# Gate products with 32 weight columns held still, conversion work behind attention on VectorE, and a longer hold for urgent work

## The chip, the cores and the metric

The kernel runs on one NeuronCore of one Trainium2 chip. Times are device microseconds (us) of that core. Engines are TensorE (PE, with its weight loads PEld), VectorE (DVE), ScalarE (ACT), GpSimd (POOL) and SyncE (SP), which issues most DMAs; POOL issues the indirect ones.

## The reference

Three layers follow one another on 3072 tokens of width 512.

```python
# 1. attention, 4 x 8 heads x 768 x 64: a local window of |i-j| < 16 and 24 block keys (max of k, mean of v over 32)
a = softmax(concat([masked scale*q@k.T, scale*q@k_sum.T + log(32)]))
x = (a @ concat([v, v_sum])).reshape to (3072, 512)
# 2. experts: 8 of them, each takes exactly 384 tokens
logits = x @ w_gate                       # 3072 x 8
# all (token, expert) pairs in falling order of logit; a token goes to the first expert that still has room
out[mask_e] = relu(x[mask_e] @ w1[e]) @ w2[e]
# 3. a dense block
h = ((out @ W1) * (out @ W2)) @ w3 @ w_out
```

## The kernel before

The program is one long stream of operations that a planner in the kernel (class `Plan`) puts in order before anything is emitted. Each operation has a due time (`with at(t)`), a duration from `cost()`, and dependencies. `run()` walks a clock: an engine that is free takes the ready operation with the earliest due time, provided that its buffers are free. Operations recorded under `urgent()` are in `hots`; an engine doesn't start other work that would still run when an urgent operation, known to become ready within `HOLD`, wants it. Buffers are given back some time after their last use: `REL` (100 ns) in general, but longer for VectorE operations that are not urgent and touch a tile named `rt` (factor on `SAFE`, 600 ns). On TensorE a change of the array's mode (full, or narrow column tiles) costs `PEN` in due time. What comes out is a fixed order for each engine; on the chip each engine runs its own list in order.

Stages. **Attention**: 16 units `u` of one batch and two heads, each with three groups `group(G)`; on TensorE every group has scores, transposes of the exponentials, products with v, and transposes `xo` into `xt`. In each third group the gate logits are accumulated: `rt` collects `xt` times `wg`, 128 tokens by 8 experts in each of six tiles, over four units; then `LG` takes them. Beside this, `conv()` turns pieces of 64-bit float weights into float32 (two 512-column halves for each 128 rows): an absolute value and a rescaling on ScalarE, a clamp on GpSimd, a shift and a merge on VectorE, an integer addition on GpSimd. `split_sb` splits a float32 tile into a rounded part (ScalarE) and the rest (GpSimd by default); `split_ps` does the same out of PSUM with VectorE.

**Transition**: when the last logits are in `LG`, `routing(0)` finds the threshold of the first expert in six rounds (VectorE compares: `gq`; TensorE counts: `rt`; VectorE: `need`, `sat`, `ni`, `base`, `thr`, `pre`), then the list of its tokens (`idx`). `fold(i)` multiplies a transposed block of w3 (`mm<-ident,w`) by w_out (`ac<-wh,xh` and so on) and keeps the product; one fold may run before the last logits and seven run behind them, as TensorE's filler. In the same stretch the dense block's first two weight matrices are made ready: tiles `ab`, half of them reloaded from `abd` (`load_ab`), half converted there (`conv_ab`).

**Experts**: 8 times. Gather the tokens (`xg`, transposed and split into `xh`, `xl`), gather w1 (`ra`) and w2 (`st`, two buffers shared with the staging of `conv`), two layers (`mm<-xh,wh`, `ac<-hh,wh`), the dense block (`mm<-xh,ab`, `ac<-w,hh`) and a scatter, while `routing(e+1)` runs among the products.

`nc.bar` is the operation that closes attention's pool; code recorded after it sees `nc.bar` set, code before it sees `None`.

Of the kernel before, what the change touches and what calls it, by code (L numbers as in the profile page):

```python
# [8 lines left out]
F32 = mybir.dt.float32  # L9
F32R = mybir.dt.float32r  # L10
BF = mybir.dt.bfloat16
I32 = mybir.dt.int32
U32 = mybir.dt.uint32
AF = mybir.ActivationFunctionType
OP = mybir.AluOpType
# [84 lines left out]
class Plan:  # L100
# [130 lines left out]
    def run(self):  # L231
# [20 lines left out]
        t, order, ends, todo = self.clock, [], [], n - base  # L252
        busy = {e: 0.0 for e in ready}
        while todo:
            moved = False
            for e, (wait, q) in ready.items():
                while wait and wait[0][0] <= t:
                    i = heapq.heappop(wait)[1]
                    heapq.heappush(q, (ops[i][5], i))
                if self.free.get(e, 0.0) > t:  # L260
                    continue
                soon = min((w[0] for w in wait if w[1] in self.hots and w[0] < t + HOLD), default=None)
                skip, got = [], None
                if e == "tensor" and q:

                    q[:] = [(ops[i][5] + PEN * (i < self.bar and self.modes.get(i) != self.mode), i) for _, i in q]
                    heapq.heapify(q)
                while q:
                    x = heapq.heappop(q)
                    late = soon is not None and x[1] not in self.hots and t + ops[x[1]][6] > soon  # L270
                    if not late and all(self.room(b) for b in ops[x[1]][4]):
                        got = x[1]
                        break
                    skip.append(x)
                for x in skip:
                    heapq.heappush(q, x)
                if got is None:
                    continue
                i = got
                dur, post = ops[i][6], ops[i][7]  # L280
                for b in ops[i][4]:
                    self.take(b)
                if e == "tensor" and i < self.bar and self.modes.get(i) != self.mode:
                    self.mode = self.modes.get(i)
                    dur += SWITCH
                self.free[e], done = t + dur, t + dur
                busy[e] += dur
                if post:

                    self.dma = max(self.dma, done + DMA_LEAD) + post  # L290
                    done = self.dma + DMA_END
                    if e == "sync":
                        self.free[e] = max(t + dur, self.dma - DMA_AHEAD)
                slow = e == "vector" and i not in self.hots and any(b.name == "rt" for b in ops[i][3])
                heapq.heappush(ends, (done + (SAFE if slow else REL), i))
                order.append(i)
                self.done[i] = t
                todo -= 1
                moved = True
                for j in users.get(i, ()):  # L300
                    kind = ops[j][2][i]
                    if kind == 0:
                        settle(i, j, t)
                    else:
                        late = self.bar is not None and j > self.bar
                        safe = 0.0
                        if e != ops[j][0] and not late:
                            safe = SAFE_A.get(ops[j][0], SAFE_O) + (SAFE_D if post else 0.0)
                        elif e != "tensor" and ops[j][0] == "tensor":
                            safe = SAFE  # L310
                        if j in self.calms and e != ops[j][0]:
                            safe = max(safe, (CALM_D if post else CALM) * (0.3 if late else 1.0))
                        settle(i, j, done + safe + (0.0 if post else LAG[e].get(ops[j][0], 0.0)))
            if moved:
                continue
            nxt = [x for x in self.free.values() if x > t] + [w[0][0] for w, _ in ready.values() if w and w[0][0] > t]
            if ends:
                nxt.append(ends[0][0])
            assert nxt, "the plan is stuck"
            t = max(t, min(nxt))  # L320
            while ends and ends[0][0] <= t:
                i = heapq.heappop(ends)[1]
                for b in ops[i][3]:
                    b.uses -= 1
                    b.when = t
# [6 lines left out]
        for i in order:  # L332
            eng, fn, _, _, new, _, _, _ = ops[i]
# [8 lines left out]
       "vector": {"tensor": 150, "scalar": 128, "gpsimd": 156, "sync": 120, "vector": 127},  # L342
       "gpsimd": {"tensor": 143, "scalar": 76, "vector": 80, "sync": 240}}

HOLD = 150.0

CALM, CALM_D = 500.0, 2000.0

# [2 lines left out]
SAFE = 600.0  # L351

SAFE_A, SAFE_O, SAFE_D = {"tensor": 1200.0, "sync": 2000.0}, 200.0, 1500.0
REL = 100.0
# [92 lines left out]
def body(tc, q, k, v, w_gate, w1, w2, wa, wb, w3, wo, out):  # L447
# [5 lines left out]
    nc = Plan(tc.nc)  # L453
# [3 lines left out]
    E, _, F = w1.shape  # L457
    C = N // 128
    cap = N // E
    NT, FB, DB = cap // 128, F // 128, Dm // 128  # L460
    NB, NJ, HP = S // 32, S // 64, H // 2
# [8 lines left out]
    STEP, T0, TL, TE = 3.3, 243, 271, 87  # L470
    GATE, EARLY = 1, 0.0
    NF, TR, FT, FD = 1, 2, 245, 3
    NW, ND, AB0, ABD = 8, 2, 12, 3.9
    P_LD, P_MN, P_VL, P_PUT, P_VC, P_RL, P_TR, P_N = 24, 8, 14, 6, 11, 10, 10, 2
    P_ST, P_SC, P_C0, P_C1, P_CL, P_FO, P_FS = 8, 10, 10, 15, 6, 3, 5
    P_GA, P_SU, P_RW, P_W2, P_W20, P_RO, P_WC = 20, 16, 40, 16, 6, 15, 6
# [17 lines left out]
    ap_ = pool(att, "att")  # L494
    pp = pool(st, "ps", space=PSUM)
# [6 lines left out]
    with at(-8):  # L502
        jp = ap_.tile([128, 128], I32, name="jp")
        nc.gpsimd.iota(jp, pattern=[[1, 128]], base=0, channel_multiplier=-1)
        ident = cp.tile([128, 128], F32, name="ident")
# [63 lines left out]
    with at(10):  # L569
        triu = cp.tile([128, 128], BF, name="triu")  # L570
        nc.vector.tensor_scalar(triu, jp, 0.0, None, op0=OP.is_gt)
        LG = cp.tile([128, C, E], F32, name="LG")
        WG = ap_.tile([128, DB, E], F32, name="wg")
        nc.sync.dma_start(WG, w_gate.rearrange("(c p) e -> p c e", p=128))


    def split_sb(hi, lo, raw, eng=None):
        nc.scalar.activation(hi, raw, AF.Copy)
        (eng or nc.gpsimd).tensor_tensor(lo, raw, hi.bitcast(F32), op=OP.subtract)

    def split_ps(hi, lo, ps):
        nc.scalar.activation(hi, ps, AF.Copy)
# [11 lines left out]
    def stage():  # L594
        return ep.tile([128, 1024], F32, name="st", bufs=2, fifo=True)


    stages = []

    def conv(src, r, h, dst, t, raw=None):  # L600

        with at(t - P_CL):
            if raw is None:
                stages.append(ap_.tile([128, 1024], F32, name="sta", bufs=2, fifo=True) if len(stages) % 2 else stage())
                raw = stages[-1]
            nc.sync.dma_start(raw.bitcast(I32), src[r * 128:(r + 1) * 128, h * 512:(h + 1) * 512].bitcast(I32))
        with at(t), nc.patient():
            w = raw.bitcast(I32).rearrange("p (a b) -> p a b", b=2)
            lo, hi = w[:, :, 0], w[:, :, 1]
            c = ap_.tile([128, 512], F32, name="ca", bufs=1) if nc.bar is None and len(stages) % 4 == 0 else ep.tile([128, 512], F32, name="a", bufs=3)  # L610
            nc.scalar.activation(c, hi.bitcast(F32), AF.Abs)
            nc.scalar.activation(lo, lo.bitcast(U32), AF.Copy, scale=2.0 ** -29)
            nc.gpsimd.tensor_scalar(c, c, 122879.9921875, 2.0 ** -15, op0=OP.min, op1=OP.max)
            a = c.bitcast(I32)
            nc.vector.tensor_scalar(a, a, 5, 2, op0=OP.logical_shift_left, op1=OP.logical_shift_right)
            nc.vector.scalar_tensor_tensor(a, hi, -1073741824, a, op0=OP.bitwise_and, op1=OP.bitwise_or)
            f = dst if dst is not None else c
            nc.gpsimd.tensor_tensor(f.bitcast(I32), a, lo, op=OP.add)
        return f

    WO, W3, WF = {}, {}, {}
# [1 line left out]
    for j in range(FB):  # L623
        t = P_C0 + (215 - P_C1) * j / nconv
        f = conv(wo, j, 0, None, t)
# [11 lines left out]
    for n, (m, d, h) in enumerate((m, d, h) for m in range(2) for d in range(ND) for h in range(2)):  # L637
        t = P_C0 + (215 - P_C1) * (FB + 2 * NW + n) / nconv
        f = conv((wa, wb)[m], d, h, None, t)
# [24 lines left out]
    GT, XT, XO = {}, {}, {}  # L664
# [76 lines left out]
    def group(G):  # L741
        nonlocal gate

        u, g = divmod(G, 3)
        b, pr = divmod(u, HP)
        with at(STEP * G):
            ps = pp.tile([128, 4, WC], F32, name="ac", bufs=2)
# [12 lines left out]
        with at(STEP * G + Q_E):  # L760
            s = ap_.tile([128, 4, WC], F32, name="s", bufs=4)
            for i in range(4):
                nc.scalar.activation(s[:, i, :], ps[:, i, :], AF.Exp, bias=mx[:, i:i + 1])
        with at(STEP * G + Q_T):
# [4 lines left out]
            p = PT[G % 3]  # L769
            nc.scalar.activation(p[0:WC], pt, AF.Copy)  # L770
        with at(STEP * G + Q_V):
            po = pp.tile([128, 2, 2, 65], F32, name="ac", bufs=4, first=3)
            with nc.block():
                for a in range(2):
                    for h in range(2):
                        for b2 in range(2):
                            i = 2 * a + b2
# [23 lines left out]
        if g == 2:  # L801
            with at(STEP * G + P_SC):
                if pr == 0:
                    GT[b] = pp.tile([128, 6, E], F32, name="rt", fifo=True)
                with nc.block():
                    for i in range(3):
                        for t in range(2):
                            nc.tensor.matmul(GT[b][:, 2 * i + t], XT[u, i][:, t], WG[:, pr], start=(pr == 0 and i + t == 0),
                                             stop=(pr == HP - 1 and i + t == 3))
        if pr == HP - 1 and g == 2:  # L810
            with at(STEP * G + P_SC):
                nc.vector.tensor_copy(LG[:, 6 * b:6 * b + 6, :], GT[b])

    for u in range(NU):
        prep(u)
# [505 lines left out]
```

## Time and profile before

| | |
|---|---|
| median of 3 runs | 1032.13 us (1030.18 to 1032.99) |
| the profiled execution | 1025.71 us, span 1023.9 us, mean granted clock 0.982 |
| busy, share of the span | PE 94%, PEld 86%, DVE 59%, ACT 40%, POOL 31% |
| attention (to the last `LG` copy) | 0 to 229 us |
| transition (to the first product of expert 0) | 229 to 298 us |
| experts | 298 to 1024 us, a period of 90 us |

The profile gives the time, duration and name of each instruction, and for an engine's idle time what released it. The share of busy time is a mean over stages with different limits, so the stages are read one by one. [...]

### The profile page before, as it was taken

To read this page: it belongs to the slowest core of one execution; us is meant where nothing else is said; L and a number is where in the kernel's file an instruction comes from. 1 tells how busy PE (TensorE), PEld (TensorE's weight loads), DVE (VectorE), ACT (ScalarE), POOL (GpSimd) and SP (SyncE) were. 2 spreads that over 40 slices of the span, in tenths; PEclk is the share of its full clock that TensorE was granted. 3 is DMA by queue.
4 is the path that set the end of the run, shared out by engine and by line. 5 is a ranking of instruction groups with operands and counts; after the bars stand their busy time and mean duration, and the time that the engine had idled before them with its cause. 6 is when DMAs were issued, how large, how long until landed. Compare 5 with 4: busy or idle time off the path is not lost.

```text
span 1023.9 us, 17970 instructions
## 1 busy us (share of the span) xinstructions
PE 966.9 (94%) x6827; PEld 877.7 (86%) x6827; DVE 603.9 (59%) x1620; ACT 409.8 (40%) x961; POOL 321.5 (31%) x401
## 2 busy tenths in 40 slices
PE   6798989997989999999999999999999999999995
PEld 5688978775678899989989998998999899999994
DVE  5775576858877853882685388268538726323210
ACT  5786878864343233233223323222332323223211
POOL 9986466646623221041022104102210414001001
PEclk9998999998999999999999999999999999999998
DMA  8767778772141311040131105003110405101000
GB/s 235 193 181 204 207 210 257 208 232 112 32 164 42 125 52 52 1 165 31 33 121 54 52 2 165 32 32 111 65 52 1 165 21 165 42 11 52 1 1 31
DMA packets 81703, 100.06 MB, mean 98 GB/s; under 512 B 30416, under 2 KB 63696, under 8 KB 81616
## 3 DMA queue, kind: packets, MB, share of 16 engines
q1 hardware_dynamic: 68560, 52.76, 18.3%
q0 software_dynamic: 13056, 46.14, 13.6%
q8 instruction: 54, 0.88, 0.3%
q14 instruction: 33, 0.27, 0.1%
HBM read 81.81 MB, written 14.68 MB: 94 GB/s over the span
## 4 chain that ended last, share of the span: by engine, by line
PE 57%; issue 10%; DVE 7%; DMA 4%; ACT 2%; POOL 2%; POOLq 0%; ACTq 0%; SPq 0%; DVEq 0%
PE mm L395 32%; PE ac L395 23%; DMA ra<-in_moe_w_dram,iw 3%; PE rt L395 2%; POOL ra L1109 1%; DVE wl L395 1%; DVE gq L395 1%; DVE a L395 1%; DVE xl L395 1%; DMA abd<-ca 1%; ACT s L395 1%; DMA st<-in_moe_w_dram,iw 1%; DVE base L395 1%; ACT wh L395 1%; DVE pre L395 0%
## 5 line engine op out<-in xcount | busy, mean ns | idle before, releaser
L395 PE MATMUL mm<-xh,ab 128*128 128x384 f32 x1024 | 273.4, 338 | 0.0
L395 PEld LDWEIGHTS mm<-xh,ab 128*128 128x128 f32 x1024 | 185.5, 188 | 4.5 <-issue 3.3
L395 PE MATMUL mm<-xl,ab 128*128 128x384 f32 x512 | 174.4, 341 | 0.0
L395 PE MATMUL ac<-w,hh 128*128 128x512 f32 x384 | 123.6, 398 | 0.0
L395 DVE TENSOR_TENSOR a<-a,mm 128x384 f32<-128x384 f32 x64 | 35.2, 551 | 140.4 <-PE mm L395 117.9
L1109 POOL DMA_INDIRECT ra<-in_moe_w_dram,iw x32 | 31.4, 982 | 219.3 <-DVE go L395 190.9
L395 PEld LDWEIGHTS mm<-xl,ab 128*128 128x128 f32 x512 | 96.1, 188 | 3.0 <-DVE xl L395 1.1
L395 PE MATMUL mm<-xh,wh 128*128 128x384 f32 x256 | 88.1, 345 | 0.8 <-ACT xh L395 0.7
L395 PE MATMUL mm<-xl,wh 128*128 128x384 f32 x256 | 87.0, 340 | 0.0
L395 PE MATMUL ac<-hl,wh 128*128 128x384 f32 x256 | 87.0, 340 | 0.0
L395 PE MATMUL ac<-hh,wl 128*128 128x384 f32 x256 | 86.8, 339 | 0.0
L395 PE MATMUL mm<-xh,wl 128*128 128x384 f32 x256 | 86.6, 338 | 0.0
L395 ACT ACTIVATE a<-mm 128x384 f32<-128x384 f32 x64 | 31.3, 490 | 137.6 <-PE mm L395 137.6
L1109 POOL DMA_INDIRECT xg<-xd,idx x24 | 35.3, 1472 | 158.6 <-PE mm L395 119.4
L395 PE MATMUL ac<-hh,wh 128*128 128x384 f32 x256 | 84.5, 337 | 0.0
L1171 POOL DMA_INDIRECT out_dram<-a,idx x24 | 26.7, 1114 | 176.9 <-ACT a L395 173.7
L395 PEld LDWEIGHTS ac<-w,hh 128*128 128x128 f32 x384 | 70.9, 188 | 11.8
L395 ACT ACTIVATE hh<-a 128x384 fp32r<-128x384 f32 x64 | 33.5, 524 | 115.7 <-DVE a L395 115.7
L395 DVE TENSOR_TENSOR wl<-st,wh 128x512 fp32r<-128x512 f32 x64 | 44.0, 688 | 57.7 <-ACT wh L395 57.5
L395 PE MATMUL ac<-w,hl 128*128 128x512 f32 x192 | 76.4, 398 | 0.0
L395 DVE TENSOR_TENSOR wl<-ra,wh 128x512 fp32r<-128x512 f32 x64 | 43.9, 687 | 41.7 <-ACT wh L395 41.7
L395 ACT ACTIVATE wh<-ra 128x512 fp32r<-128x512 f32 x64 | 42.4, 664 | 62.2 <-PE mm L395 32.7
(271 smaller groups left out, 2078.8 us busy)
## 6 DMA issues: line engine op xcount, KB each, us to landing
st<-in_moe_w_dram SPq DMA_DIRECT2D x14, 512.0 KB
sta<-in_moe_w_dram SPq DMA_DIRECT2D x14, 512.0 KB
kn<-in_k_dram SPq DMA_DIRECT2D x32, 192.0 KB
qn<-in_q_dram SPq DMA_DIRECT2D x32, 192.0 KB
xd<-xo SPq DMA_DIRECT2D x16, 384.0 KB
vw<-in_v_dram SPq DMA_DIRECT2D x32, 176.0 KB
vw<-vs SPq DMA_DIRECT2D x64, 36.6 KB
st<-in_moe_w_out_dram SPq DMA_DIRECT2D x4, 512.0 KB
```

The lines of the kernel that those rows point to most:

```text
L395: return getattr(real_engine, method)(*map(real, a), **{k: real(x) for k, x in kw.items()})
L1109: nc.add("gpsimd", lambda: tc.nc.gpsimd.indirect_dma_start(out=real(dst), out_offset=None, in_=real(src), in_offset=bass.IndirectOffsetOnA ...
L1171: s = tc.nc.gpsimd.indirect_dma_start(out=out, out_offset=bass.IndirectOffsetOnAxis(ap=real(idx), axis=0), in_=real(o), in_offset=None)
```

## The change

1. The gate logits are computed with `wg` held still (each of the four 128-row pieces padded from 8 to 32 columns with zeros) and 256 tokens of `xt` streaming: three products for each unit, into three bands of 32 partitions. Before, six products held 128x128 of `xt` still and streamed 8 columns. After four units, ScalarE copies the 96 rows out (`lt`), TensorE transposes them in two pieces, and VectorE copies the first 8 columns of each band to `LG`.
2. Code recorded after `nc.bar` gives the rests of `split_sb` and the final addition of `conv` to VectorE. Its staging uses `st` alone, where `sta` (attention's pool) alternated with it.
3. `AB0`, the first due time of the `ab` work relative to `T0`, goes from 12 to 22. `HOLD` goes from 150 to 300 ns, and `rt` tiles of VectorE operations that are not urgent are given back after 1800 instead of 600 ns.

```diff
-                heapq.heappush(ends, (done + (SAFE if slow else REL), i))
+                heapq.heappush(ends, (done + (3 * SAFE if slow else REL), i))
...
-HOLD = 150.0
+HOLD = 300.0
...
-    NW, ND, AB0, ABD = 8, 2, 12, 3.9
+    NW, ND, AB0, ABD = 8, 2, 22, 3.9
...
-        WG = ap_.tile([128, DB, E], F32, name="wg")
-        nc.sync.dma_start(WG, w_gate.rearrange("(c p) e -> p c e", p=128))
+        WG = ap_.tile([128, DB, 32], F32, name="wg")
+        nc.gpsimd.memset(WG, 0.0)
+        nc.sync.dma_start(WG[:, :, 0:E], w_gate.rearrange("(c p) e -> p c e", p=128))
...
-        (eng or nc.gpsimd).tensor_tensor(lo, raw, hi.bitcast(F32), op=OP.subtract)
+        (eng or (nc.gpsimd if nc.bar is None else nc.vector)).tensor_tensor(lo, raw, hi.bitcast(F32), op=OP.subtract)
...
-                stages.append(ap_.tile([128, 1024], F32, name="sta", bufs=2, fifo=True) if len(stages) % 2 else stage())
+                stages.append(ap_.tile([128, 1024], F32, name="sta", bufs=2, fifo=True) if nc.bar is None and len(stages) % 2 else stage())
...
-            nc.gpsimd.tensor_tensor(f.bitcast(I32), a, lo, op=OP.add)
+            (nc.gpsimd if nc.bar is None else nc.vector).tensor_tensor(f.bitcast(I32), a, lo, op=OP.add)
...
-                    GT[b] = pp.tile([128, 6, E], F32, name="rt", fifo=True)
+                    GT[b] = pp.tile([128, 256], F32, name="rt", fifo=True)
                 with nc.block():
                     for i in range(3):
-                        for t in range(2):
-                            nc.tensor.matmul(GT[b][:, 2 * i + t], XT[u, i][:, t], WG[:, pr], start=(pr == 0 and i + t == 0),
-                                             stop=(pr == HP - 1 and i + t == 3))
+                        nc.tensor.matmul(GT[b][32 * i:32 * i + 32], WG[:, pr], XT[u, i].rearrange("p t s -> p (t s)"),
+                                         start=(pr == 0), stop=(pr == HP - 1))
         if pr == HP - 1 and g == 2:
             with at(STEP * G + P_SC):
-                nc.vector.tensor_copy(LG[:, 6 * b:6 * b + 6, :], GT[b])
+                lt = ap_.tile([96, 256], F32, name="lt", bufs=1)
+                nc.scalar.activation(lt, GT[b][0:96], AF.Copy)
+                ps = pp.tile([128, 2, 96], F32, name="mm", bufs=3)
+                for t in range(2):
+                    nc.tensor.transpose(ps[:, t, :], lt[:, t * 128:(t + 1) * 128], ident[0:96, 0:96])
+                nc.vector.tensor_copy(LG[:, 6 * b:6 * b + 6, :].rearrange("p (g t) e -> p g t e", t=2),
+                                      ps.rearrange("p t (g r) -> p g t r", r=32)[:, :, :, 0:E])
```

How the order of the engines moves is shown at three places. TensorE at the end of attention, before; `ac` with `xh`, `xl` is a fold, `rt<-wg,xt` a pair of gate products, `mm<-ident,w` a fold's transposes:

```order
L395 MATMUL ac_3477<-wl_1246,xh_3394 128x512
L395 MATMUL rt_3172<-wg_155,xt_3490 128x8 x2
L395 MATMUL rt_3172<-wg_155,xt_3508 128x8 x2
L395 MATMUL rt_3172<-wg_155,xt_3534 128x8 x2
L395 MATMUL ac_3477<-wh_1220,xl_3395 128x512
L395 MATMUL mm_3562<-ident_88,w_1_1496 128x128 x4
```

The same place with the change:

```order
L395 MATMUL ac_3382<-wh_1268,xl_3222 128x512
L395 MATMUL rt_3140<-xt_3437,wg_347 32x256
L395 MATMUL rt_3140<-xt_3465,wg_347 32x256
L395 MATMUL rt_3140<-xt_3483,wg_347 32x256
L395 MATMUL mm_3504<-ident_88,lt_3499 128x96 x2
L395 MATMUL mm_3526<-ident_88,w_1_1533 128x128 x4
```

Three products stand for six, and the two transposes of `lt` follow them at once, ahead of the next fold. The first fold's last product stands before the logits now.

VectorE in the second round of `routing(0)`, before (`a<-ab,a` is a conversion's merge, `w` a fold's result):

```order
L395 TENSOR_TENSOR gq_3697<-key_3574,thr_3692 128x768
L395 TENSOR_TENSOR gq_3705<-key_3574,thr_3692 128x768
L395 TENSOR_TENSOR w_1_3708<-ac_3598,w_1_3708 128x512
L395 TENSOR_TENSOR need_3738<-rem_1046,rt_3715 32x8 x2
L395 TENSOR_TENSOR sat_3743<-rt_3715,need_3738 63x8
L395 TENSOR_REDUCE ni_3754<-rt_3751 128x1
```

With the change (`ab` minus `ab` is the rest of a gate weight):

```order
L395 TENSOR_TENSOR gq_3621<-key_3509,thr_3616 128x768
L395 TENSOR_TENSOR gq_3631<-key_3509,thr_3616 128x768
L395 TENSOR_TENSOR ab_0_3537<-ab_0_3537,ab_0_3599 128x512
L395 TENSOR_SCALAR a_3628<-a_3628 128x512
L395 TENSOR_TENSOR need_3662<-rem_791,rt_3640 32x8 x2
L395 TENSOR_TENSOR sat_3669<-rt_3640,need_3662 63x8
L395 TENSOR_TENSOR w_1_3665<-ac_3564,w_1_3665 128x512
L395 TENSOR_REDUCE ni_3682<-rt_3679 128x1
```

A rest and a conversion's shift now stand between the comparison and `need`, and the fold's result after `sat`. From the `LG` copy to `idx` twelve such rests and additions are new in VectorE's list; a conversion and a half, and two folds' results, have left that stretch.

GpSimd as expert 0 begins, before (`xg` gathers tokens, `st` gathers w2, `a` is a conversion, `ab` a rest):

```order
L1109 DMA xg_4248<-xd,idx_4193 128x512
L1109 DMA st_4273<-in_moe_w_dram,iw_0_4049 128x1024
L395 TENSOR_SCALAR a_4378<-a_4378 128x512
L395 TENSOR_TENSOR a_4378<-a_4378,st_4336 128x512
L1109 DMA st_4428<-in_moe_w_dram,iw_0_4049 128x1024
L395 TENSOR_TENSOR ab_0_3730<-a_4378,ab_0_3713 128x512
```

With the change:

```order
L1115 DMA xg_4184<-xd,idx_4123 128x512
L1115 DMA st_4222<-in_moe_w_dram,iw_0_3974 128x1024
L1115 DMA st_4282<-in_moe_w_dram,iw_0_3974 128x1024
L395 TENSOR_SCALAR a_4417<-a_4417 128x512
L395 TENSOR_SCALAR a_4515<-a_4515 128x512
L395 TENSOR_SCALAR a_4552<-a_4552 128x512
L395 TENSOR_SCALAR a_4650<-a_4650 128x512
```

The fourth gather of w2 now goes ahead of all conversions, and four conversions stand here, where two stood: the other two were done in attention before, through `sta`. SP loads their four pieces last of all.

## Rows read from the trace of the kernel before

**Rows 1.** Busy time by stretch: us, PE, PEld, DVE, ACT, POOL, clock, DMA.
```profile
50.00:220.00 170.00, 156.85 (x1874) 138.76 (x1874) 116.05 (x235) 136.54 (x414) 110.09 (x151) 0.95 0.76 209
229.00:298.00 69.00, 57.56 (x321) 41.38 (x322) 61.85 (x143) 30.92 (x55) 38.62 (x32) 0.95 0.31 111
298.00:337.00 39.00, 36.62 (x228) 35.19 (x228) 26.83 (x86) 13.06 (x25) 7.73 (x7) 0.96 0.15 45
427.00:517.00 90.00, 89.49 (x548) 82.84 (x547) 55.80 (x176) 26.29 (x51) 16.18 (x17) 1.00 0.19 65
```
**Rows 2.** Timeline of PE in attention: start, us, instruction, count, idle before.
```profile
53.03 0.49 PE L395 MATMUL mm<-ident,qr 128*128 128x128 f32 x3
53.36 0.38 PE L395 MATMUL mm<-ident,xo 128*128 128x128 f32 x2
...
57.55 1.40 PE L395 MATMUL rt<-wg,xt 128*128 128x8 f32 x12
...
60.42 0.55 PE L395 MATMUL mm<-ident,kr 128*128 128x128 f32 x3
60.90 0.88 PE L395 MATMUL mm<-vw,ind 96*32 96x130 f32 x24
...
64.02 1.05 PE L395 MATMUL ac<-kw,qb 128*128 128x120 f32 x8
```
**Rows 3.** Timeline of DVE in `routing(0)`.
```profile
229.14 0.21 DVE L395 COPY LG<-rt 128x48 f32<-128x48 f32 x1 [3.95 <-PE rt L395]
...
236.47 1.18 DVE L395 TENSOR_SCALAR a<-a 128x512 int32<-128x512 int32 x1
...
239.84 0.91 DVE L395 SCALAR_TENSOR_TENSOR base<-tb,u 128x1 int32<-128x1 int32 x1
240.79 1.26 DVE L395 TENSOR_TENSOR thr<-js,base 128x64 int32<-128x64 int32 x1
241.97 1.26 DVE L395 TENSOR_TENSOR pre<-js,base 128x32 int32<-128x32 int32 x1
243.15 3.36 DVE L395 TENSOR_TENSOR gq<-key,thr 128x768 bf16<-128x768 f32 x2
...
250.81 0.16 DVE L395 SCALAR_TENSOR_TENSOR base<-ni,base 128x1 int32<-128x1 int32 x1
...
251.11 0.19 DVE L395 TENSOR_TENSOR pre<-js,base 128x32 int32<-128x32 int32 x1
251.22 0.95 DVE L395 TENSOR_TENSOR gq<-key,thr 128x768 bf16<-128x768 f32 x1
...
269.32 1.26 DVE L395 SCALAR_TENSOR_TENSOR base<-ni,base 128x1 int32<-128x1 int32 x1
...
287.58 0.15 DVE L395 SCALAR_TENSOR_TENSOR idx<-i 128x3 int32<-128x3 f32 x1
```
**Rows 4.** Timeline of POOL in the same stretch.
```profile
240.69 1.27 POOL L395 TENSOR_TENSOR ab<-ab,ab 128x512 fp32r<-128x512 f32 x1
241.92 1.26 POOL L395 TENSOR_TENSOR ab<-a,ab 128x512 fp32r<-128x512 f32 x1
```
**Rows 5.** Timeline of PE in the transition.
```profile
245.29 0.33 PE L395 MATMUL rt<-oh,gq 128*128 128x16 bf16 x6 [5.04 <-DVE gq L395]
...
297.77 1.41 PE L395 MATMUL mm<-xh,wh 128*128 128x384 f32 x3 [0.69 <-ACT xh L395]
```
**Rows 6.** Groups by line and shape: instruction, count, busy us, mean ns, idle before.
```profile
L395 DVE TENSOR_TENSOR wl<-st,wh 128x512 fp32r<-128x512 f32 x64 | 44.0, 688 | 57.7 <-ACT wh L395 57.5
L395 ACT ACTIVATE xt<-mm 128x256 f32<-128x256 f32 x48 | 19.3, 403 | 2.8 <-PE mm L395 2.7
L395 POOL TENSOR_TENSOR ab<-ab,ab 128x512 fp32r<-128x512 f32 x8 | 11.2, 1410 | 7.0 <-ACT ab L395 7.0
L395 POOL TENSOR_SCALAR a<-a 128x512 f32<-128x512 f32 x32 | 21.6, 679 | 28.0 <-ACT a L395 20.4 <-DVE thr L395 5.4 <-DVE rs L395 0.9
```
**Rows 7.** Timeline of ACT and of PE in expert 0.
```profile
318.56 1.15 ACT L395 ACTIVATE wh<-st 128x512 fp32r<-128x512 f32 x2 [4.67 <-DMA st<-in_moe_w_dram,iw]
322.22 0.31 PE L395 MATMUL rt<-oh,gq 128*128 128x16 bf16 x6 [1.36 <-DVE gq L395]
```

## The prediction

> **What bounds the kernel now.** I read the busy time by stretch first, then the engines' timelines in the stretches that are not full, then the groups of instructions for prices. The stretches [rows 1] show three regimes. In a steady expert TensorE is busy 89.49 of 90 us: nothing in the change alters its products, so 7 of the 8 periods are taken as they are. In attention (50 to 220 us) TensorE is busy 156.85 of 170 us, 92%, with ScalarE next at 136.54 us, 80%: here TensorE's own work sets the pace, not quite alone. In the transition (229 to 298 us) TensorE is busy 57.56 of 69 us and VectorE 61.85: the chain of `routing(0)` on VectorE is the longer one. It starts with the `LG` copy at 229.14 and gives `idx` at 287.58, 58.4 us later [rows 3]; the first product of expert 0 follows at 297.77, 10.2 us on [rows 5], behind the gather of tokens. The expert-0 stretch of 39 us has 2.4 us of idle TensorE (39.00 - 36.62) [rows 1].
>
> **The gate products.** A unit's batch takes 1.40 us on TensorE now [rows 2], in 12 records, which are six float32 products. It comes 16 times. What replaces it isn't in the trace, so I bound it by two rows. The block means use the same kind of narrow tile, 32 columns held still: 12 products of 130 columns, 1560 columns in all, take 0.88 us [rows 2]. Four bands work there, three will here; 3 x 256 = 768 columns cost 0.88 x 768/1560 x 4/3 = 0.58 us. If the bands do not overlap, the full-width float32 row decides: 4 products of 120 columns in 1.05 us [rows 2], so 768 columns cost 1.05 x 768/480 = 1.68 us.
>
> A switch between the full and the narrow form also shows: three transposes reach the next instruction after 0.33 us elsewhere (53.03 to 53.36), but after 0.48 us when the narrow means follow (60.42 to 60.90) [rows 2], 0.15 us. So a batch saves 1.40 - 0.58 - 0.15 = 0.67 us, 16 of them 10.7 us; at the other end it costs 1.68 + 0.15 - 1.40 = 0.43 us more, 6.9 us in all. I take the row of the means, because its instruction has the same narrow form. [...]
>
> What of 10.7 us reaches the end? TensorE was idle 8% of the stretch, and ScalarE at 80% goes to about 85% when the stretch shrinks. I pass on a good half: **-6 us**, with 0 and -10.7 as ends of this term if the tiles overlap. The clamp, addition and load of two conversions also leave attention for expert 0; they are off its critical engine there, so I give them nothing here.
>
> **The logits' way out.** Three of the four copies stand inside attention, with other work queued on TensorE between product and transpose. The last one is on the path: where `LG` followed the product at once, there are now a copy on ScalarE (0.40 us by the nearest row, `xt` with 256 columns [rows 6]), two transposes (0.33 us for three of 128 [rows 2], so about 0.25) and two more hand-overs. I put **+1 us** on it. TensorE stands still meanwhile, since the transposes are next in its list; ends +0.7 and +1.5.
>
> **The transition.** Between 236.47 and 269.32 eleven VectorE instructions of the chain and of the conversions (first and last shown, the worst four between) take 15.6 us [rows 3]. The same forms take 0.16 us (`base`), 0.19 (`pre`), 0.95 (`gq`) when nothing disturbs them [rows 3]; summed that way the eleven would take 4.4 us. Each long one ends with a two-input GpSimd instruction: `thr` at 240.79 and `pre` at 241.97 run beside `ab` at 240.69 and 241.92 [rows 3, 4]. So 11.2 us of the chain are waits for GpSimd. The costliest is the second round, where TensorE stands 5.04 us for `gq` [rows 5]. [...]
>
> The change takes those GpSimd instructions (1410 ns each [rows 6]) out of the stretch. In their place twelve of VectorE's own stand in the list from `LG` to `idx`, at 688 ns each (`wl`, same shape and operands [rows 6]): 12 x 0.69 = 8.3 us. One and a half conversions and two fold results leave it (some 2.9 us at 0.4 to 0.7 us each). One end: all that is added lies on the chain, -11.2 + 8.3 = -2.9 us. Other end: the added ones fill the places where VectorE waited for a count from TensorE, and the chain falls by 11.2 and nearly all the rest is free: -12 us. [...] I take **-9 us**: 69 becomes 60.
>
> Four clamps stay on GpSimd in this stretch (679 ns [rows 6]). [...]
>
> **Expert 0.** The wait of ScalarE for the fourth piece of w2, 4.67 us, and TensorE's 1.36 us behind it [rows 7] should go, since that gather is issued ahead of the conversions now. In its place VectorE gets two more whole conversions, and the additions and rests of four: 4 x 2 x 0.69 + 2 x 1.1 = 7.7 us in a stretch where it was busy 26.83 of 39 us [rows 1]. It becomes nearly full, in front of counts that TensorE waits for in order. I put **+1 us** (-2.4, all idle time gone, to +5). `HOLD` and the longer life of `rt` act only on the plan; with TensorE at 99% in the experts I give them zero, ends -1 and +2.
>
> **Sum.** -6 + 1 - 9 + 1 = -13 us. The profiled execution took 1025.71 us, its span and 1.8 us around it; it would become 1012.7. The median of the runs is 6.4 us longer (1032.13). I carry the difference over to the median: **1019 us**.
>
> **Rivals.**
> *Attention keeps its pace* (0.15). ScalarE, the loads and GpSimd set it, and TensorE only idles more. For it: ScalarE's 80%; against: TensorE's 92%. Then 1032.1 + 0 + 1 - 9 + 1 = 1025.
> *VectorE's newcomers take back the transition* (0.15). They stand in front of `need` and `ni` rather than beside a wait. For it: VectorE is busy 61.85 of 69 us; against: a good part of that was waiting. Term -2.9: 1025.
> *The bands do not overlap* (0.08), so the change does not do what it says: +6.9 in attention. For it: no row with 256 columns. Then 1032.1 + 6.9 + 1 - 9 + 1 = 1032, no change.
> *Slower: conversions block VectorE in expert 0* (0.10). Their four pieces go through the two `st` buffers behind w2, and VectorE's list has their shifts in front of `gq` and `hl`, for which TensorE waits. If each arrives as late as w2's fourth piece did, 4.67 us [rows 7], that is 18.7 us: 1032.1 - 6 + 1 - 9 + 18.7 = 1037. It decides for "slower" from 4.3 us a piece (to make up 14 us and 3 more). Against it: the loads are issued when w2's halves are split, several products ahead.
> *My forecast* has 0.52, with its own range 1012 to 1025.
>
> **How the numbers follow.** About 0.3%, 3 us, is what a measurement of this kernel can tell from no change. Forecast and the first two rivals lie below 1029: 0.82, of which I hold back 0.02 for their upper tails. The third gives 0.08, with a little from the others 0.09; slower 0.11. The range reaches down for the unknown costs (-10.7 and -12 together give 1011, with no loss in expert 0 1009) and up over the two rivals at 1025: 1009 to 1030.
>
> **What would show it.** The gate products in three records' worth of 256 columns at about 0.6 us a batch; the `LG` copy some 5 us earlier, near 224; in `routing(0)` `base`, `thr` and `pre` at 0.2 us each, no TensorE wait of 5 us, `idx` about 49 us behind `LG`; first product of expert 0 near 284; expert period 90.0 as before. The forecast is wrong if the batches still take 1.4 us, if VectorE waits in expert 0 for a conversion's shift, or if the stretch from `LG` to `idx` stays above 55 us.

## The result: 1002 us, and the profile after

The changed kernel takes 1002.35 us, the median of 4 runs (999.45 to 1003.75), beside 1031.16 (1028.75 to 1032.99) for 4 runs of the kernel before: ratio 0.9718, 95% interval 0.9687 to 0.9749. The forecast was 1019 us with a range of 1009 to 1030. The direction was right, and the time lies below the range: the gain is 29 us by the medians where I had 13.

The profiled execution took 999.45 us, with a span of 997.7, 26.2 us under the span before. (Both profiled executions are faster than their medians, that of the kernel before by 5.5 us and this one by 2.9, so the spans show a smaller gain.) The mean granted clock is 0.990 (before 0.982). TensorE is busy 95% of the span, VectorE 61%, ScalarE 41%, GpSimd 28%. Split at the same five points the 26.2 us are:

| stretch | before, us | after, us | difference | forecast |
|---|---|---|---|---|
| start to the last `LG` copy | 229.1 | 215.9 | -13.2 | -5 |
| `LG` copy to `idx` | 58.4 | 49.4 | -9.0 | -9 for both |
| `idx` to the first product of expert 0 | 10.2 | 11.3 | +1.1 | |
| from there to expert 0's first product with `ab` | 39.4 | 36.2 | -3.2 | +1 |
| from there to the end | 686.7 | 684.9 | -1.8 | 0 |

Busy time by stretch, after (us, then PE, PEld, DVE, ACT, POOL, and clock, DMA share, GB/s), against [rows 1]:

```profile
50.00:207.00 157.00, 141.97 (x1815) 117.93 (x1815) 111.71 (x223) 134.02 (x407) 103.31 (x135) 1.00 0.79 218
216.00:276.00 60.00, 54.31 (x310) 39.74 (x310) 55.76 (x150) 27.23 (x51) 15.22 (x15) 0.97 0.41 141
276.00:312.00 36.00, 34.51 (x218) 33.08 (x219) 30.83 (x83) 16.27 (x30) 3.45 (x5) 1.00 0.29 89
402.00:492.00 90.00, 89.99 (x550) 83.62 (x549) 56.37 (x179) 26.65 (x51) 14.75 (x17) 1.00 0.20 65
```

In attention the clock column reads 1.00 where it read 0.95. In a steady expert TensorE is busy 89.99 of 90 us where it was busy 89.49.

TensorE in attention, after (start, us, instruction, count), against the batch in [rows 2]:

```profile
55.63 0.88 PE L395 MATMUL mm<-vw,ind 96*32 96x130 f32 x24
56.32 0.61 PE L395 MATMUL rt<-xt,wg 128*32 128x256 f32 x6
56.86 0.98 PE L395 MATMUL mm<-ident,xo 128*128 128x128 f32 x4
...
213.06 0.63 PE L395 MATMUL rt<-xt,wg 128*32 128x256 f32 x6
214.56 0.39 PE L395 MATMUL mm<-ident,lt 96*128 96x96 f32 x2 [0.86 <-ACT lt L395]
214.78 1.04 PE L395 MATMUL mm<-ident,w 128*128 128x128 f32 x8
```

A batch is recorded with 0.61 us, and the next instruction starts 0.54 us behind its start. From 213.06 on stands the logits' way out: TensorE waits 0.86 us for ScalarE's copy `lt`, transposes it, and goes on with a fold.

VectorE from the last logits to the third round of `routing(0)`, after, against [rows 3]:

```profile
214.87 0.42 DVE L395 TENSOR_SCALAR ca<-ca 128x512 int32<-128x512 int32 x1
215.32 0.69 DVE L395 SCALAR_TENSOR_TENSOR ca<-sta,ca 128x512 int32<-128x512 int32 x1
215.93 0.20 DVE L395 COPY LG<-mm 128x48 f32<-128x48 f32 x1
...
225.47 0.16 DVE L395 SCALAR_TENSOR_TENSOR base<-tb,u 128x1 int32<-128x1 int32 x1
225.66 0.23 DVE L395 TENSOR_TENSOR thr<-js,base 128x64 int32<-128x64 int32 x1
225.81 0.19 DVE L395 TENSOR_TENSOR pre<-js,base 128x32 int32<-128x32 int32 x1
225.92 1.83 DVE L395 TENSOR_TENSOR gq<-key,thr 128x768 bf16<-128x768 f32 x2
227.67 0.69 DVE L395 TENSOR_TENSOR ab<-ab,ab 128x512 fp32r<-128x512 f32 x1
...
229.19 0.34 DVE L395 TENSOR_TENSOR need<-rem,rt 32x8 f32<-32x8 f32 x2 [0.50 <-PE rt L395]
...
231.00 0.48 DVE L395 SCALAR_TENSOR_TENSOR base<-ni,base 128x1 int32<-128x1 int32 x1
...
242.56 0.49 DVE L395 TENSOR_TENSOR pre<-js,base 128x32 int32<-128x32 int32 x1
...
265.31 0.15 DVE L395 SCALAR_TENSOR_TENSOR idx<-i 128x3 int32<-128x3 f32 x1
```

`base`, `thr` and `pre` take 0.16 to 0.23 us where they took 0.91 to 1.26, and the rest of a gate weight (`ab<-ab,ab`, 227.67) lies ahead of a wait that VectorE would have had anyway. On TensorE the wait of 5.04 us [rows 5] is gone. GpSimd, against [rows 4], has one two-input addition left there, at the very start and still from attention, and four clamps, of which the last three are shown:

```profile
216.15 1.28 POOL L395 TENSOR_TENSOR ca<-ca,sta 128x512 int32<-128x512 int32 x1 [2.23 <-ACT xh L395]
...
230.86 0.62 POOL L395 TENSOR_SCALAR a<-a 128x512 f32<-128x512 f32 x1 [5.88 <-DMA ab<-in_moe_w_dram]
239.62 0.62 POOL L395 TENSOR_SCALAR a<-a 128x512 f32<-128x512 f32 x1 [8.14 <-ACT a L395]
242.39 0.62 POOL L395 TENSOR_SCALAR a<-a 128x512 f32<-128x512 f32 x1 [2.16 <-ACT a L395]
```

Beside that addition one long row of the old kind is left on VectorE:

```profile
216.56 1.10 DVE L395 TENSOR_TENSOR eq<-LG,key 128x192 f32<-128x192 f32 x1
```

The same instruction took 0.36 us in the kernel before (at 229.77), with no GpSimd instruction beside it. So some 0.7 us of the old loss is still in the changed kernel.

### The profile page after: what moved, and what is told of

Same layout as the page of the kernel before. It is cut to its first block, busy times and chain, and to the rows that moved or that the text cites. A ratio compares the mean times of both kernels' runs of the same rounds, so it can differ in the third digit from the quotient of the medians.

```text
span 997.7 us, 17811 instructions
## 1 busy us (share of the span) xinstructions
PE 947.3 (95%) x6739; PEld 853.0 (85%) x6739; DVE 608.3 (61%) x1644; ACT 411.6 (41%) x965; POOL 279.7 (28%) x378
## 4 chain that ended last, share of the span: by engine, by line
PE 70%; issue 9%; DVE 8%; DMA 4%; ACT 4%; POOL 3%; SPq 0%; POOLq 0%; ACTq 0%; DVEq 0%
PE mm L395 38%; PE ac L395 31%; PE rt L395 2%; DMA vw<-in_v_dram 1%; DVE a L395 1%; DVE gq L395 1%; ACT s L395 1%; DMA xg<-xd,idx 1%; POOL vw L395 1%; DMA vw<-vs 1%; DVE xl L395 1%; DVE ca L395 1%; DVE mx L395 1%; DMA kn<-in_k_dram 1%; DVE kw L395 1%
## 5 line engine op out<-in xcount | busy, mean ns | idle before, releaser
L395 PE MATMUL mm<-xh,ab 128*128 128x384 f32 x1024 | 276.8, 339 | 0.0
L395 PE MATMUL ac<-w,hh 128*128 128x512 f32 x384 | 120.2, 394 | 0.0
L1115 POOL DMA_INDIRECT xg<-xd,idx x24 | 24.2, 1007 | 147.5 <-PE mm L395 112.6
L395 ACT ACTIVATE wh<-st 128x512 fp32r<-128x512 f32 x64 | 40.4, 632 | 53.3 <-PE ac L395 26.9
```

The lines of the kernel that those rows point to most:

```text
L395: return getattr(real_engine, method)(*map(real, a), **{k: real(x) for k, x in kw.items()})
L1115: nc.add("gpsimd", lambda: tc.nc.gpsimd.indirect_dma_start(out=real(dst), out_offset=None, in_=real(src), in_offset=bass.IndirectOffsetOnA ...
```

## The experiments

In the text, "wide" products are the six of the kernel before and "narrow" ones the three of the change. Medians are of 4 to 10 runs, ratios are to the kernel before on the same chip (1029.36 for the first four kernels, 1029.09 for the last four), with 95% intervals. The four runs `replan_...` are single ones. A stretch or a busy time is that of the one profiled execution of each kernel. "Expert 0's first half" is the time from the first product of expert 0 to its first product with `ab`.

**One part alone.** The kernel before with the narrow products. It has the staging through `st` alone too, as has the fourth kernel below.

```diff
+        WG = ap_.tile([128, DB, 32], F32, name="wg")
...
+                        nc.tensor.matmul(GT[b][32 * i:32 * i + 32], WG[:, pr], ...)
```

> The kernel before with the narrow gate products (and with staging behind attention on st alone, which they need); GpSimd keeps the additions and rests, HOLD, AB0 and the rt factor are as before. Theory (the products' saving passes whole through attention): the LG copy comes near 216 us as with the whole change, LG to idx stays near 58 us with the long base, thr and pre, total about 1018. Rival (the gain in attention needs the other parts' plan): LG stays above 222, total 1025 or more.

1014.13 us, ratio 0.9845 (0.9807 to 0.9884). `LG` comes at 218.98, `LG` to `idx` stays at 55.9 us. The narrow products alone bring half of the gain, in the profiles all of it ahead of `LG` (218.98 for 229.14, with a span 9.9 us shorter).

The kernel before with additions and rests on VectorE (edit 2 of the change):

```diff
...
-            nc.gpsimd.tensor_tensor(f.bitcast(I32), a, lo, op=OP.add)
+            (nc.gpsimd if nc.bar is None else nc.vector).tensor_tensor(f.bitcast(I32), a, lo, op=OP.add)
```

> The kernel before with only the additions and rests behind attention on VectorE. Theory (the waits of VectorE for GpSimd are the transition's loss): LG near 229, LG to idx falls from 58.4 to about 50, total about 1022. Rival (the later AB0 and the longer HOLD made the transition shorter): LG to idx stays at 56 or more, total 1029 to 1033.

1022.9 us, ratio 0.9934 (0.9903 to 0.9966). `LG` at 230.54, `LG` to `idx` 50.7 us (before 58.4): the transition's gain is this part's. Expert 0's first half grows to 41.4 us (39.4), with a TensorE wait of 2.59 us for `gq`, so part of the gain is given back there.

The kernel before with the three plan numbers:

```diff
-HOLD = 150.0
+HOLD = 300.0
...
-    NW, ND, AB0, ABD = 8, 2, 12, 3.9
+    NW, ND, AB0, ABD = 8, 2, 22, 3.9
...
-                heapq.heappush(ends, (done + (SAFE if slow else REL), i))
+                heapq.heappush(ends, (done + (3 * SAFE if slow else REL), i))
```

> The kernel before with only the plan's numbers: HOLD 300, AB0 22, rt given back after 1800 ns. Theory: the waits for GpSimd stay, LG to idx 55 to 60 us, total within 4 us of 1031. Rival (the numbers made the transition shorter): LG to idx near 50, total about 1022.

1021.75 us, ratio 0.992 (0.9894 to 0.9947). The stretch from the first product with `ab` to the end falls to 682.8 us (686.7), `LG` to `idx` to 55.8 (58.4; two other orders of the kernel before, below, have 56.2 and 56.1, so this fall need not be the numbers'). A part that I had given nothing is worth 8 us by the ratio.

**The changed kernel less one part.** With the additions and rests back on GpSimd:

```diff
...
-            (nc.gpsimd if nc.bar is None else nc.vector).tensor_tensor(f.bitcast(I32), a, lo, op=OP.add)
+            nc.gpsimd.tensor_tensor(f.bitcast(I32), a, lo, op=OP.add)
```

> The changed kernel with the additions and rests behind attention back on GpSimd (staging on st alone stays). Theory: LG near 216, LG to idx back to 56 to 60 us, total about 1012. Rival (VectorE's new work cost as much as the waits): LG to idx near 50, total 1002 to 1005.

1013.19 us, ratio 0.983 (0.9788 to 0.9871): `LG` at 216.81, but 56.3 us from `LG` to `idx` and 45.0 us in expert 0's first half. The long rows on VectorE are back, beside GpSimd's two-input instructions again:

```profile
227.83 1.29 DVE L395 TENSOR_TENSOR thr<-js,base 128x64 int32<-128x64 int32 x1
...
254.04 1.30 DVE L395 SCALAR_TENSOR_TENSOR base<-ni,base 128x1 int32<-128x1 int32 x1
```

```profile
227.76 1.28 POOL L395 TENSOR_TENSOR ab<-ab,ab 128x512 fp32r<-128x512 f32 x1
...
254.01 1.31 POOL L395 TENSOR_TENSOR a<-a,ab 128x512 int32<-128x512 int32 x1 [0.89 <-DVE ni L395]
```

`thr`, at 0.23 us undisturbed, ends with the `ab` instruction of GpSimd (229.12 and 229.04), as it did in [rows 3, 4]. This is the mechanism of the transition, shown by putting it back.

Without the plan numbers (`HOLD` 150, `AB0` 12, `SAFE` once):

> The changed kernel without the three plan numbers (HOLD 150, AB0 12, rt tiles given back after 600 ns). Theory: the plan numbers keep TensorE of the steady experts full: without them busy 444 to 447 of 450 us, first product with ab to the end 687 to 690 us instead of 684.9; LG and the way from LG to idx as in the changed kernel (216 to 219, 49 to 51); time 1005 to 1009. Rival, as I had predicted (zero in the experts): 684 to 686 us, time 1001 to 1004.

1005.94 us, ratio 0.978 (0.9757 to 0.9802), `LG` at 215.99, 50.9 us from `LG` to `idx`, and 686.5 us from the first product with `ab` to the end. Steady TensorE falls to 447.52 of 450 us. I had expected 444 to 447 us busy and 687 to 690 us for that stretch: the direction came, a little smaller. The ratio lies 0.006 above the change, some 6 us. The two spans differ by 4.0 us, spread over `LG` to `idx`, expert 0 and the experts, and a new order alone moves as much in these stretches.

Without the narrow products:

> The kernel before with the additions and rests on VectorE and the plan numbers, so the changed kernel without the narrow gate products. If the three parts add up, 1029.4 less 6.5 (additions on VectorE) and 7.6 (plan numbers) = 1015, LG at 229 to 231, 49 to 51 us from LG to idx, 449.9 of 450 us busy in the steady experts; the narrow products are then worth 12 to 13 us in the full change too. Rival, the first two parts share one gain: 1019 to 1022. Rival, half passed on in attention: LG near 222, time 1008.

1015.88 us, ratio 0.9879 (0.9856 to 0.9903). `LG` is back at 228.57. The ratios lie 0.016 apart with the change, some 16 us, so the narrow products are worth as much in the full change as alone. The staging is the same in both, so it has no part in these 16 us.

**How much does a new order alone move?** Each edit lets the planner order everything anew. A due time that no edit of the change touches was shifted, in the kernel before and in the changed one:

```diff
-    SWITCH, PEN = 150.0, 3.0
+    SWITCH, PEN = 155.0, 3.0
```

(155 in `replan_b1` and `replan_a1`, 160 in `replan_b2`, 145 in `replan_a0`.)

> The kernel before, planned again with SWITCH 155 instead of 150 ns: nothing else differs but the order. Theory (the products made attention shorter): LG between 225 and 232 us. [...]

> The kernel before, planned again with SWITCH 160 instead of 150 ns. [...]

> The changed kernel, planned again with SWITCH 145 instead of 150 ns. Theory: LG between 213 and 219 us, LG to idx 47 to 52 us, total 999 to 1006. Rival (a lucky order): LG up to 225 us, total up to 1015.

> The changed kernel, planned again with SWITCH 155 instead of 150 ns. As for 145: by the theory LG between 213 and 219 us and total 999 to 1006, by the rival LG up to 225 and total up to 1015.

1029.62 and 1029.69 us for the kernel before (its own single run there 1031.82), 1002.74 and 1001.78 for the changed one. `LG` at 231.35 and 231.45, and at 217.59 and 217.52. A new order moves `LG` by some 2 us. (The totals are single runs and tell little: 15 runs of the kernel before lie between 1024.87 and 1035.16.) It moves other stretches too: in the kernel before `LG` to `idx` is 56.2 and 56.1 us, where it was 58.4, and from the first product with `ab` to the end 690.8 and 690.9, where it was 686.7. So one pair of profiles is not enough for a part of this size, but all 14 kernels together are. `LG` to `idx` is 48.2 to 51.0 us in the seven with the additions and rests on VectorE and 55.8 to 58.4 in the seven without. That another order spares TensorE the falls of its clock did not show: the two new orders of the kernel before have a clock of 0.94 and 0.95 behind 50 us, as it has itself (0.95). Two orders are few to exclude it.

**Is product time in attention passed on?** The changed kernel with every narrow product issued twice; its logits are doubled.

```diff
-                    for i in range(3):
+                    for i in range(6):
...
```

> The changed kernel with each narrow gate product issued twice into the same sums (the logits come out doubled, which this run does not care for). 16 batches get three more products each; a batch of three took 0.61 us. Theory A, attention passes TensorE's product time on whole: 16 x 0.61 = 9.8 us, the last LG copy from 215.9 to about 225.5, time from 1002.4 to about 1012. Rival B, a good half is passed on, as I had predicted: LG near 221, time near 1007.5. Rival C, the gain in attention came from stalls and clock falls that went, and not from the products' time: LG stays within 2 us (the size of a re-planning), time 1001 to 1005.

1009.01 us, ratio 0.9797 (0.9764 to 0.9829), so 0.008 above the change, about 8 us. With 0.003 of error on each ratio this cannot tell whole (6.9 us by the records below) from half; the profile has to. `LG` moves from 215.93 to 228.56, and more than the added products is in it. A batch's record grows from 0.61 to 1.04 us, 16 x 0.43 = 6.9 us, and the clock falls come back. TensorE from 50 us to `LG`, in the changed kernel and then in this one:

```profile
50.00:215.93 165.93, 149.93 (x1873) 123.55 (x1871) 117.79 (x234) 138.78 (x417) 107.99 (x140) 1.00 0.78 218
```

```profile
50.00:228.56 178.56, 161.85 (x1974) 133.16 (x1973) 123.82 (x236) 140.97 (x419) 110.17 (x150) 0.97 0.75 210
```

Clock 0.97 over 178.56 us is an estimated 5.4 us lost ((1 - clock) x time, 0.03 x 178.56), and 6.9 + 5.4 = 12.3 of the 12.6 us. TensorE's idle time is 16.0 us in the one and 16.7 in the other: it took up nothing. My theory of a good half (`LG` at 221) falls, and so does the third, by which `LG` would have stayed. The first one, the whole, had `LG` at 225.5 and named no clock.

**Which plan number fills the experts?** The kernel before with the longer life of `rt` alone:

```diff
-                heapq.heappush(ends, (done + (SAFE if slow else REL), i))
+                heapq.heappush(ends, (done + (3 * SAFE if slow else REL), i))
```

> The kernel before with only the longer life of rt tiles (1800 instead of 600 ns). Theory: this number alone fills TensorE in the steady experts, since its waits for rt buffers go: busy 449 to 450 of 450 us (446.9 before), first product with ab to the end 683 to 685 us (686.7 before), time 1025 to 1027. Rival: HOLD does it, and this run stays at 446 to 447 us busy, 686 to 691 us, time 1028 to 1031.

1023.51 us, ratio 0.994 (0.9924 to 0.9957). Five periods of TensorE, in the kernel before and in this one:

```profile
400.00:850.00 450.00, 446.87 (x2726) 413.87 (x2725) 278.22 (x882) 131.16 (x250) 81.02 (x85) 1.00 0.20 65
```

```profile
400.00:850.00 450.00, 449.94 (x2745) 418.31 (x2744) 279.15 (x885) 133.33 (x253) 79.18 (x88) 1.00 0.20 66
```

And TensorE's waits in these 450 us of the kernel before (releaser, us in total, times, longest):

```profile
PE rt L395 <- DVE i L395: 3.0, 5, 0.8
```

That line is gone with this one number, as it is in the changed kernel. In each of the five periods one product into `rt` had stood where it waited for VectorE's read `i` of such a tile, 0.6 us on average; now it stands later. The idle time falls by 3.07 us, and the first product with `ab` to the end by 3.3 (686.7 to 683.4). The theory holds: it is this number, and `HOLD` isn't needed for it. An order alone moves this busy time too (443.9 us in both new orders of the kernel before, where TensorE waits for `gq`), but over all kernels the number decides: 449.8 to 449.9 us in the eight that have it, 443.9 to 447.5 in the six that don't. The median fell by more, 5.6 us; the profiled execution has its `LG` at 233.14 and 11.0 us lost to the clock in attention, so it is no guide to the other 2 us.

## Why the prediction was wrong

Two steps failed, both in attention: the share of the products' saving, and the clock, which had no term. Up to `LG` I forecast -5 us (-6 + 1), and it became -13.2. TensorE to `LG`, in the kernel before and then in the changed one (its rows behind 50 us stand above):

```profile
0.00:50.00 50.00, 34.92 (x349) 29.67 (x350) 31.66 (x77) 31.95 (x94) 45.72 (x85) 0.99 0.79 217
50.00:229.14 179.14, 165.99 (x1941) 146.55 (x1941) 118.82 (x240) 139.24 (x419) 113.31 (x154) 0.95 0.77 212
```

```profile
0.00:50.00 50.00, 35.46 (x337) 29.82 (x338) 32.94 (x80) 32.62 (x97) 45.18 (x94) 0.93 0.75 208
```

Its busy time falls from 200.9 to 185.4 us, by 15.5, and its idle time grows from 28.2 to 30.5, by 2.3. The clock loss, estimated as (1 - clock) x time, is 0.5 + 9.0 us before and 3.5 + 0.0 after: some 6 of the 15.5 us are the clock, and the rest, some 9.5, is work that TensorE no longer does.

**The first step that failed: "I pass on a good half: -6 us".** The price of a batch was about right. Before, it mostly took 1.26 us from start to next start:

```profile
84.63 1.40 PE L395 MATMUL rt<-wg,xt 128*128 128x8 f32 x12
85.89 0.63 PE L395 MATMUL ac<-ident,s 128*120 128x128 f32 x4
```

After, the four batches that stand right behind the block means (as at 56.32) take 0.54 us, and the means ahead of them 0.70 to the next start instead of 0.80. The other twelve take 0.56, and what stands ahead of them gets some 0.10 us longer (the scores at 124.84: 0.98 us to the batch at 125.82, where scores with a full-form instruction behind them, take 0.88). That is 4 x 0.82 + 12 x 0.60 = 10.5 us saved, where the forecast had 10.7; the transposes of `lt` take back some 0.9. The share was wrong: idle time, which was to take up nearly half of the saving, took up at most the 2.3 us by which it grew, and 0.86 of these are the wait for `lt`. The kernel without narrow products and the changed one with another order, at nearly equal clock losses behind 50 us, show the same:

```profile
50.00:228.57 178.57, 162.22 (x1944) 142.47 (x1943) 117.84 (x236) 137.73 (x416) 109.98 (x151) 0.98 0.75 208
```

```profile
50.00:217.59 167.59, 151.84 (x1866) 125.14 (x1866) 115.06 (x235) 137.77 (x416) 111.09 (x140) 0.98 0.76 213
```

TensorE's busy time falls by 10.4 us and `LG` comes 11.0 us earlier; idle time is 16.4 and 15.8 us. (Some 2 us of this are the clock's: ahead of 50 us it is 0.93 in the first and 0.97 in the second.) ScalarE has the same 137.7 us in both, 77% and 82%, without setting the pace. I had read TensorE's 8% idle as slack that takes up part of a saving. It is made of short waits (before and after none above 1.7 us, and some 70% of the time is for ScalarE's results) and stayed at 13 to 17 us behind 50 us in every kernel here. The end -10.7 of this term was the right value.

**The second step, and in this pair of profiles the larger: the clock in attention, a term that I had not written.** [Rows 1] show 0.95 over 170 us, and none of my terms has it. Its 6 us are about what the time lies below my range. Three stretches of 6 us in the kernel before, and the same times of the changed one:

```profile
90.00:96.00 6.00, 4.10 (x26) 3.65 (x24) 4.23 (x7) 4.84 (x18) 4.47 (x7) 0.81 0.41 85
96.00:102.00 6.00, 6.00 (x57) 5.25 (x57) 2.44 (x5) 1.99 (x6) 4.00 (x5) 0.50 0.98 272
102.00:108.00 6.00, 6.00 (x82) 5.16 (x82) 2.43 (x6) 3.67 (x12) 0.81 (x2) 0.84 0.67 190
```

```profile
90.00:96.00 6.00, 5.45 (x84) 4.05 (x79) 3.83 (x10) 4.62 (x14) 5.75 (x7) 1.00 0.77 237
96.00:102.00 6.00, 6.00 (x73) 5.42 (x72) 3.14 (x6) 4.94 (x18) 2.31 (x5) 1.00 0.82 225
102.00:108.00 6.00, 4.95 (x42) 4.51 (x40) 4.90 (x9) 5.17 (x21) 4.61 (x9) 1.00 0.39 77
```

Before the fall, TensorE waits and then works slowly:

```profile
90.02 0.49 PE L395 MATMUL mm<-ident,qr 128*128 128x128 f32 x3
91.86 0.52 PE L395 MATMUL mm<-ident,kr 128*128 128x128 f32 x3 [1.35 <-ACT kw L395]
92.93 0.52 PE L395 MATMUL mm<-ident,qr 128*128 128x128 f32 x3 [0.55 <-ACT xt L395]
93.28 0.37 PE L395 MATMUL ac<-mv,sel 67*128 67x480 bf16 x1
93.49 1.71 PE L395 MATMUL ac<-kw,qb 128*128 128x120 f32 x8
95.00 2.58 PE L395 MATMUL rt<-wg,xt 128*128 128x8 f32 x12
```

Two waits, 1.9 us together, stand ahead of the fall of the granted clock (0.81 in these 6 us, 0.50 in the next); then the scores take 1.71 us and a batch 2.58 (1.05 and 1.40 in [rows 2], where the clock is 1.00). By the same estimate the three stretches lose 0.19, 0.50 and 0.16 of their 6 us, 5.1 us in all. From the start to `LG` the loss is 9.5 us before and 3.5 after. Over all profiles it is 7.1 to 14.5 us in the seven with wide products, 3.5 to 5.2 in the six with narrow ones, and 8.4 with the narrow ones doubled. So the narrow products take some falls away, but how many varies from kernel to kernel. Whether the shorter batches themselves prevent falls, or only the order that follows from them, stays open. How much of a clock loss reaches `LG` isn't shown either: of the seven kernels with wide products, the one that lost least (7.1 us) was idle for 31.6 us up to `LG`, and one that lost 14.4 for 28.1.

**The logits' way out (+1)** was too cheap. From the end of the last batch (213.69) to the `LG` copy it took 2.2 us, where the copy had followed at once. About 1 us of it is not the copy and the transposes but two conversion instructions that stand ahead of `LG` in VectorE's list (214.87 and 215.32). TensorE did a fold's transposes beside it.

**The transition (-9)** held in place and cause, and in this pair in size: `LG` to `idx` 49.4 us against "about 49", the wait of 5.04 us gone, and -7.9 us with the gather behind it, which is 1.1 us slower. (The first product of expert 0 is at 276.63 and not near 284, since `LG` is earlier.) That the size fits so well is in part luck: against the other two orders of the kernel before the gain from `LG` to `idx` is some 7 us. Where the -9 lies between its ends, -2.9 and -12, was an estimate of mine that no row showed. Beside two of the four clamps an instruction of the chain was long: `base` beside the clamp at 230.86 (0.48 for 0.16 us) and `pre` beside that at 242.39 (0.49 for 0.19), 0.6 us in all. `base` ends with its clamp, at 231.48, `pre` with its own (243.05 and 243.01), and `eq` (216.56), 1.10 us for 0.36, ends 0.23 us behind the two-input addition at 216.15.

**Expert 0 (+1)** came out at -3.2. The wait for w2's fourth piece and its 1.36 us on TensorE are gone, as forecast, and nearly nothing came in their place. TensorE's waits from 276 to 318 us (releaser, us in total, times, longest):

```profile
PE mm L395 <- ACT xh L395: 0.7, 1, 0.7
PE rt L395 <- DVE gq L395: 0.6, 2, 0.4
PE ac L395 <- DVE hl L395: 0.4, 1, 0.4
```

VectorE is busy 30.83 of 36 us and no conversion's shift is late enough to be waited for. My end -2.4 (all idle time gone) left out the clock: 0.96 over 39 us is 1.6 us, and it is 1.00 now. The size is in part the order's: the changed kernel has 36.2, 38.1 and 36.2 us in its three orders, the kernel before 39.4, 39.9 and 39.9. No part brings it alone: 41.4 us with the VectorE part, 39.7 with the plan numbers, 38.6 with the narrow products; without the VectorE part it is 45.0 us, at a clock of 0.90 and with 6.1 us of idle TensorE (45.05 - 38.91). Which instruction's place does it isn't shown.

**The plan numbers (0)** were a misreading of a row that was there. [Rows 1] had 0.51 us of idle time in a steady expert of 90 us; seven of these are 3.6 us, with TensorE as the only bound, and I called 89.49 full. The runs give 3.3 us for the life of `rt` in the kernel before, in its own order; over all kernels that stretch is 682.8 to 685.2 us with the longer life and 686.5 to 690.9 without. In the changed kernel the numbers are worth 1.6 us of span there (686.5 without them, 684.9 with them), and steady TensorE again goes from 447.52 to 449.93 of 450 us.

**The rivals and the range.** None of the four came. A batch is recorded with 0.61 us, not with the 1.68 that I had estimated for bands that do not overlap, attention does not keep its pace, VectorE's newcomers do not stand in the way, and no conversion blocks expert 0. The case that I had left out was a gain well beyond my forecast. The lower end of the range was also badly summed: -10.7 and -12 with nothing for expert 0 give 1010.4, not 1009, and with every term at its good end (-10.7 + 0.7 - 12 - 2.4 - 1) it is 1006.7. The measured 1002.35 lies below even that: the clock in attention, with no term, was missing from every end.

## What to carry to other kernels

Where one engine sets the pace of a stretch (here TensorE at 92%, the next at 80%, and 10.4 us less of its busy time brought `LG` 11.0 us earlier), pass a saving of its time on whole, until a row names the engine that ends its waits after the change. A clock under 1.00 in a stretch is a term of the sum in that stretch, and a half microsecond of idle time in a repeated stage is multiplied by the number of stages. Before a gain is put down to an edit in a planned kernel, run the plan with an unrelated number shifted: here that moved `LG` and each stretch by some 2 us and the experts by 4, and the parts moved the whole by 6 to 16.

## What the runs showed of the hardware

Three more narrow products in the same form cost 0.43 us (`gates_twice`, a record of 1.04 for 0.61), where the first three behind the block means cost 0.54 to the next start (56.32 to 56.86): by this estimate the change out of the narrow form takes about 0.11 us. The change into it, estimated from the instruction ahead, is some 0.10 us (the scores at 124.84, 0.98 for 0.88). Both are less than the 0.15 us for one switch that I took from [rows 2]. The twelve batches away from the block means have both. And 6.9 us of added products in attention moved `LG` by 12.6, nearly twice that, with an estimated 5.4 us lost to the clock beside them in that execution.

In the rows with GpSimd's additions back (`no_vec_st`) two VectorE instructions that began beside a two-input GpSimd instruction of 128x512 (1.28 and 1.31 us) ended within 0.1 us of it: `thr` (128x64), 1.29 us for 0.23, and `base` (128x1), 1.30 for 0.16.
